# Block 1's VectorE and ScalarE work held in program order, with one weight tile rounded earlier and part of w_in's sums on GpSimd

## The chip, the cores and the metric

The kernel runs on one NeuronCore of a Trainium2 chip. TensorE (PE, with its weight loads as PEld) multiplies, VectorE (DVE), ScalarE (ACT) and GpSimd (POOL) do the rest, and SyncE (SP) issues most DMAs. The metric is device time in microseconds; smaller is better. A difference below 0.3% can't be told from none.

## What is computed

Linear attention without softmax, normalised per row, followed by a two-layer network with a leaky ReLU:

```python
kv = np.einsum('bhsd,bhse->bhde', k, v)        # batch 8, heads 8, seq 576, dim 64
out = np.einsum('bhsd,bhde->bhse', q, kv)
rms = np.sqrt(np.mean(out * out, axis=-1, keepdims=True) + 1e-06)
x = (out / rms * g_norm)                       # then (B,H,S,D) -> (4608, 512)
h = x @ w_in                                   # 512 x 2048, float64 in memory
g = np.maximum(0.01 * h, h)
return g @ w_out                               # 2048 x 512, float64 in memory
```

q, k, v are float32. The two weight matrices come as float64, and the kernel rounds them to float32 itself.

## The kernel before

**Blocks, chunks and slots.** The 4608 rows are nine blocks of 512. The 2048 hidden columns are four chunks (NC = 4), each of two pairs of 128 columns from the lower and the upper half. Block 0 goes first, while weights arrive: `first_block` multiplies chunks 0 to 2 directly, in 12 steps n; step n makes one product with w_in (`h_ps`), applies the leaky ReLU on ScalarE (L1140), and multiplies the result of step n-1 with w_out into four accumulators. Between these, `between(n, 0)` and `between(n, 1)` run what the table `plan` lists for (n, 0) and (n, 1): a number is a weight tile to round, `f` finishes the roundings begun, `t` is a step of the attention of block 0's last rows, `a` a step of block 1's attention, `x` makes block 1's four x sums.

Then comes block 1 with all four chunks, then block 0's chunk 3, then blocks 2 to 8. From here each chunk's two layers are products by Strassen's scheme (seven products instead of eight of half size). Block 1 and block 0's chunk 3 are five units `now` = 0 to 4, each of seven slots, `at` = 7*now + t, 0 to 34. In a slot TensorE makes one first-layer product (8 matmuls of 128x256) and, from slot 9 on, one second-layer product of an earlier unit. First-layer products come in the order 1, 2, 6, 5, 7, 3, 4 and alternate between two banks (h_a and h_c in even units, h_b and h_d in odd ones). A product that accumulates on a bank, or starts it anew, must wait until the last result there has been copied (ScalarE) or added (VectorE): `done` in `product_h`. The seven sides of each product are sums that GpSimd makes: `sides_w1` of w_in, `sides_w2` of w_out, `sums_of` of the activations (tiles gs). Product 6 of the second layer needs the second gs sum.

For blocks 2 to 8 the scheme is applied twice to the first layer, and the weights for that, 49 pieces a chunk, are made once in slots of block 1 and written to DRAM: `combine(c, part)`. Parts 0 and 1 take the sums that `sides_w1` made, parts 2 and 3 w_in's own quarters. The sums of parts 0 and 1 run on GpSimd, those of 2 and 3 on VectorE. `put_off` delays a write by some slots, and `READS` says when the first five pieces are read back into w_in's place (a ring).

**Rounding.** Each of 32 weight tiles (128x512) is loaded raw (512 KB) into one of a few raw homes and rounded in three ScalarE and three VectorE steps that alternate: two reads (L263, L261), a clip (VectorE, L265), ScalarE L270, VectorE L280 and L283. Tiles 24 to 31 are chunk 3's; their homes are the two halves of `early` and the first part of `stage`, in turn. Tiles up to 26 are rounded in `first_block`, the others in slots 0 to 14, one in three slots.

**What sets the order.** The program is traced in one order, and a planner then orders each engine's instructions by its own model of time. An instruction that is pinned stays behind the one traced just before it on its engine. Matmuls, DMAs and roundings are pinned everywhere; in `first_block` attention's work is too, from block 2 on everything; in block 1 (`in_block_1`, set once and never cleared) only GpSimd's sums and the few adds that say so. Block 1's copies, ReLUs and attention steps are the planner's to place. The x sums of block 1 are made in `first_block` and aren't pinned. GpSimd's first instruction after it (L1194) reads the last x sum, so that its sums don't start earlier.

Of the kernel before, what the change touches and what calls it, by code (L numbers as in the profile page):

```python
# [24 lines left out]
def kernel(  # L25
# [70 lines left out]
    def in_turn(ins):  # L96

        if steady or in_line or in_first:
            pin(ins)

    def first_turn(ins):

        if in_first:
            pin(ins)
# [113 lines left out]
    def spare(n, name, dtype=F32):  # L218
# [7 lines left out]
        itertools.cycle([early[:, :NW], early[:, NW:], raws[0]]))  # L226
# [196 lines left out]
    def divide(lo, hi, sums):  # L423
# [3 lines left out]
        for l in range(2):  # L427
# [4 lines left out]
            if l:  # L432
                if in_first:
                    yield
                act = nc.scalar.activation(rms, rms, func=AF.Sqrt, scale=1.0 / D, bias=eps_sb)
                if first_done or in_first:
                    pin(act)
# [58 lines left out]
    def attention(b, apart=True, fine=False):  # L496
# [39 lines left out]
        if KV_BESIDE <= b < B - 1:  # L536
            kv = [(None, None), (0, 1)] if b > KV_BESIDE else [(None, 0), (None, 1)]
        tails = [tail_of(b, max(i * NT, b * S), min((i + 1) * NT, (b + 1) * S),
                         fine or i == b == 1, kv[i - b]) for i in (b, b + 1)]
# [156 lines left out]
    def add(eng, out_, a, b_, minus=False, pinned=False):  # L696
        ins = eng.tensor_tensor(out_, a, b_, op=ALU.subtract if minus else ALU.add)  # L697
        if pinned or steady or (in_block_1 and eng is nc.gpsimd):
            pin(ins)
# [27 lines left out]
    def put_off(to, t):  # L727
        later.append([2 if first_done and in_loop else 1, to, t])
# [8 lines left out]
    def sides_w2(n):  # L737
# [7 lines left out]
        def sums(i):  # L745
# [15 lines left out]
            else:  # L761
# [15 lines left out]
    stage_homes = iter([view(w1_all, (6 + i) * NW, NW) for i in (0, 1)]  # L777
                       + [view(stage, i * NW, NW) for i in (1, 2, 1, 2, 0, 1, 2, 0, 1, 2, 0, 1, 2, 0)])

    def combine(c, part):  # L780
# [5 lines left out]
            [((1, 2), direct)], [((4,), last)]  # L786

        eng = nc.vector if part > 1 else nc.gpsimd
        for js, y in parts[part]:
# [4 lines left out]
            add(eng, s1, y21, y22, pinned=part > 1)  # L794
            add(eng, s2, s1, y11, True, pinned=part > 1)
            add(eng, s3, y11, y21, True, pinned=part > 1)
            add(eng, s4, y12, s2, True, pinned=part > 1)
            to = w1_dram[c][:, :, AT[js[0]]:AT[js[0]] + len(js), :]
            if js[0] == 1:
                for r in range(2):  # L800
                    put_off(to[:, r, :, :], y[:, 0, r, :, :])
            else:
                put_off(to[:, :2, :, :], y[:, 0, :, :, :])
            put_off(to[:, 2, :, :], y22)
            put_off(to[:, 3:, :, :], t)
# [103 lines left out]
    def relu(t, src=None):  # L909
        nc.scalar.activation(t, t if src is None else src, func=AF.Prelu, alpha=SLOPE)  # L910
# [17 lines left out]
    def product_h(n, w_sides, x_sides, to):  # L928
# [3 lines left out]
        def done(i, bank):  # L932

            if i == 1:
                nc.scalar.copy(g11, bank)
            elif i == 5:
                nc.scalar.copy(g22, bank)
# [3 lines left out]
            elif i == 6:  # L941
                nc.scalar.copy(g21, bank)
# [108 lines left out]
    def product_o(n, g_sides, os, finish, second):  # L1051
# [15 lines left out]
        def done(i, bank):  # L1067
# [11 lines left out]
            if c == 0 and fresh:  # L1079
                nc.scalar.copy(to, bank)  # L1080
# [41 lines left out]
    def first_block(between):  # L1122
# [27 lines left out]
        for t in range(4):  # L1150
            o = opool.tile([P, DM], F32, tag="o", name="o", bufs=6)
            if t % 2:
                nc.scalar.copy(o, accs[t])
            else:
                nc.vector.tensor_copy(o, accs[t])
# [8 lines left out]
            (7, 0): (a, a, 17, f), (7, 1): (a, 18, f), (8, 0): (a, 19, f), (8, 1): (a, 20, f),  # L1164
            (9, 0): (a, a, 21, f), (9, 1): (22, a, f), (10, 0): (a, 23, a, f), (10, 1): (a, x),
            (11, 0): (24, f), (11, 1): (25, f), (12, 1): (26, f)}
    loaded, x_sides = 12, None

    def between(n, half):
        nonlocal loaded, x_sides  # L1170
        for what in plan.get((n, half), ()):
# [7 lines left out]
            else:  # L1179
                round_w(what)  # L1180
                to = what + 7 if what < 17 else max(24, what + 3)
# [14 lines left out]
    more()  # L1196
    for part in range(2):
        combine(0, part)
    for part in range(2):
        sides_w2(0)[1](part)  # L1200
    in_loop = True

    LATE_ONE = {17: 2, 19: 1}
    A_SLOTS = {18: 1, 19: 1, 20: 1, 23: 1, 24: 1, 25: 1, 26: 1, 27: 1, 28: 1, 29: 1, 34: 2}
    DIRECT = {15: 0, 16: 1, 20: 2, 21: 3, 22: 4, 23: 5, 26: 6, 27: 7}
    READS = {20: 2, 24: 4, 28: RING}
# [27 lines left out]
    for i, chunks in rounds:  # L1234
        one = i < 2
# [6 lines left out]
        for c in chunks:  # L1242
# [5 lines left out]
            for t in range(7):  # L1248
# [46 lines left out]
                if one:  # L1295
                    if at in DIRECT:
                        combine(DIRECT[at] // 2, 2 + DIRECT[at] % 2)
# [12 lines left out]
                    if loaded < min(rounded + 3, len(w_jobs)):  # L1310
# [6 lines left out]
                    load_some()  # L1317
                    if at == 7 * NC - 4:
                        x_sides, _, sums, _ = sides_x(0)
                    elif at == 7 * N1 - 4:  # L1320
                        x_sides, new_quarters, sums, inner = sides_x(2)
                    if at in (7 * NC - 4, 7 * NC - 3, 7 * N1 - 4, 7 * N1 - 3):
                        go(sums, 2)
                    if at == 7 * N1 - 3:
                        inner(0)
                    elif at == 7 * N1 - 2:
# [45 lines left out]
```

## Time and profile before

| what | us |
|---|---|
| median of 3 runs (lowest, highest) | 930.14 (929.48, 931.88) |
| the profiled execution's own time | 931.65 |
| its span, first to last instruction | 929.9 |
| mean granted TensorE clock | 0.993 of full |

The span is what the profile covers; the execution around it adds 1.75 us. The page lists busy time per engine, then the span in 40 slices. Some landmarks of its timeline: block 0's dense products begin at 23 us, block 1's first product at 111.1 us, block 0's chunk 3 at 216.1 us, block 2 at 242.2 us. One Strassen product, 8 matmuls of 128x256, takes 1.725 us from start to start; a step of `first_block`, 8 matmuls of 128x512, 3.43 us.

### The profile page before, as it was taken

To read this page: it belongs to the slowest core of one execution; us is meant where nothing else is said; L and a number is where in the kernel's file an instruction comes from. 1 tells how busy PE (TensorE), PEld (TensorE's weight loads), DVE (VectorE), ACT (ScalarE), POOL (GpSimd) and SP (SyncE) were. 2 spreads that over 40 slices of the span, in tenths; PEclk is the share of its full clock that TensorE was granted. 3 is DMA by queue.
4 is the path that set the end of the run, shared out by engine and by line. 5 is a ranking of instruction groups with operands and counts; after the bars stand their busy time and mean duration, and the time that the engine had idled before them with its cause. 6 is when DMAs were issued, how large, how long until landed. Compare 5 with 4: busy or idle time off the path is not lost.

```text
span 929.9 us, 18153 instructions
## 1 busy us (share of the span) xinstructions
PE 911.9 (98%) x7024; PEld 788.7 (85%) x7024; DVE 632.4 (68%) x1151; ACT 347.7 (37%) x679; POOL 375.8 (40%) x443
## 2 busy tenths in 40 slices
PE   8999979989999999999999999999999999999998
PEld 5544467878898999999999999999999999999997
DVE  5765855959575877577856786688658755765565
ACT  5756444213234422433333324333343333223330
POOL 2000299844622275226422632255225622552322
PEclk9999989999999999999999999999999999999999
DMA  8997283997689678867886779757765676667632
GB/s 256 249 246 194 68 277 119 278 310 226 207 263 333 203 231 249 256 226 227 250 260 227 219 218 256 243 174 217 242 184 173 188 226 198 185 187 220 199 118 91
DMA packets 92405, 202.16 MB, mean 217 GB/s; under 512 B 10016, under 2 KB 44448, under 8 KB 92320
## 3 DMA queue, kind: packets, MB, share of 16 engines
q1 hardware_dynamic: 81344, 189.14, 68.4%
q10 hardware_dynamic: 10528, 10.69, 3.4%
q8 instruction: 56, 0.92, 0.4%
q0 software_dynamic: 448, 1.18, 0.3%
q14 instruction: 29, 0.24, 0.1%
HBM read 173.44 MB, written 27.53 MB: 216 GB/s over the span
## 4 chain that ended last, share of the span: by engine, by line
PE 85%; DMA 8%; DVE 4%; ACT 2%; issue 1%; POOL 0%; SPq 0%; ACTq 0%; DVEq 0%; POOLq 0%
PE o_c L126 19%; PE o_a L126 18%; PE h_ha L126 11%; PE h_hb L126 10%; PE h_hc L126 8%; PE h_hd L126 8%; PE o_ps L126 3%; PE h_a L126 2%; PE h_c L126 2%; DMA stage<-in_moe_w_out_dram 2%; DMA pairs<-in_moe_w_in_dram 1%; PE h_d L126 1%; PE h_b L126 1%; DMA pairs<-in_v_dram 1%; DMA pairs<-in_moe_w_out_dram 1%
## 5 line engine op out<-in xcount | busy, mean ns | idle before, releaser
L697 POOL TENSOR_TENSOR gs<-g 128x512 f32<-128x512 f32 x66 | 85.2, 1291 | 254.9 <-ACT g L910 254.9
L910 ACT ACTIVATE g<-g 128x512 f32<-128x512 f32 x127 | 80.1, 631 | 143.1 <-DVE g L697 143.1
L1029 ACT COPY w_all<-h_ha 128x512 f32<-128x512 f32 x84 | 49.0, 583 | 169.8 <-PE h_ha L126 164.1
L126 PE MATMUL o_c<-pairs,gs 128*128 128x256 f32 x392 | 93.2, 381 | 0.0
L126 PE MATMUL o_a<-pairs,gs 128*128 128x256 f32 x392 | 93.0, 380 | 0.0
L697 DVE TENSOR_TENSOR o<-h_hb,o 128x128 f32<-128x128 f32 x104 | 29.8, 287 | 83.6 <-ACT pairs L1029 83.5
L126 PEld LDWEIGHTS o_c<-pairs,gs 128*128 128x128 f32 x392 | 71.3, 190 | 9.4 <-POOL pairs L697 1.2
L126 PEld LDWEIGHTS o_a<-pairs,gs 128*128 128x128 f32 x392 | 71.3, 190 | 8.1
L697 DVE TENSOR_TENSOR o<-o_a,o 128x512 f32<-128x512 f32 (+1 forms) x93 | 62.5, 672 | 21.0 <-PE o_a L126 20.6
L697 DVE TENSOR_TENSOR o<-o_c,o 128x512 f32<-128x512 f32 x80 | 54.7, 683 | 27.5 <-PE o_c L126 26.2
L126 PE MATMUL h_ha<-stage,w_all 128*128 128x128 f32 x448 | 59.6, 276 | 0.0
L126 PEld LDWEIGHTS h_ha<-stage,w_all 128*128 128x128 f32 x448 | 56.6, 192 | 3.0 <-issue 0.7
L697 DVE TENSOR_TENSOR g<-g,pairs 128x512 f32<-128x512 f32 x84 | 55.7, 689 | 1.9
L697 POOL TENSOR_TENSOR pairs<-g 128x128 f32<-128x128 f32 x52 | 23.8, 458 | 75.8 <-PE h_hb L126 47.4
L697 DVE TENSOR_TENSOR w_all<-h_hc,w_all 128x512 f32<-128x512 f32 x56 | 38.3, 685 | 15.9 <-PE h_hc L126 15.8
L697 DVE TENSOR_TENSOR o<-h_hd,o 128x128 f32<-128x128 f32 x78 | 22.1, 283 | 38.1 <-ACT pairs L1029 38.0
L126 PE MATMUL h_hb<-stage,w_all 128*128 128x128 f32 x336 | 46.7, 275 | 0.0
L697 POOL TENSOR_TENSOR gs<-gs,g 128x512 f32<-128x512 f32 x33 | 44.3, 1341 | 2.6
L1029 ACT COPY pairs<-h_hb 128x384 f32<-128x384 f32 x84 | 40.1, 477 | 13.8 <-PE h_hb L126 12.9
L697 POOL TENSOR_TENSOR gs<-g,gs 128x512 f32<-128x512 f32 x33 | 45.2, 1369 | 0.0
L126 PE MATMUL o_acc<-w,g 128*128 128x512 f32 x96 | 43.4, 597 | 0.0
L126 PE MATMUL h_hd<-xT,w_all 128*128 128x128 f32 x224 | 43.3, 275 | 0.0
(242 smaller groups left out, 2249.7 us busy)
## 6 DMA issues: line engine op xcount, KB each, us to landing
w_all<-w SPq DMA_DIRECT2D x196, 448.0 KB, 4.2
pairs<-w SPq DMA_DIRECT2D x56, 512.0 KB, 4.3
out_dram<-o ACTq DMA_DIRECT2D x35, 256.0 KB, 4.4
v_in<-in_v_dram SPq DMA_DIRECT2D x27, 288.0 KB, 4.8
k_in<-in_k_dram SPq DMA_DIRECT2D x26, 288.0 KB, 4.4
q_in<-in_q_dram SPq DMA_DIRECT2D x52, 144.0 KB, 5.5
q_in<-in_q_dram SPq DMA_DIRECT2D x52, 140.0 KB, 5.5
w<-stage SPq DMA_DIRECT2D x10, 512.0 KB, 4.1
```

Of the source, the lines that this page charges most:

```text
L126: pin(nc.tensor.matmul(*args, **kw))
L697: ins = eng.tensor_tensor(out_, a, b_, op=ALU.subtract if minus else ALU.add)
L910: nc.scalar.activation(t, t if src is None else src, func=AF.Prelu, alpha=SLOPE)
L1029: nc.scalar.copy(q[:, at], bank)
```

## The change

In block 1 and block 0's chunk 3 (`in_block_1` is now true for these rounds alone, and cleared after them) everything on VectorE and ScalarE is pinned: copies, ReLUs, adds and attention's steps. Tile 24 is rounded in (8, 0) beside tile 19, tile 25 in (10, 1) after the x sums, tile 26 in (11, 0); block 1's attention steps 12 to 14 come one place earlier, and loads are asked for at other steps. Tiles 27 to 31 use the halves of `early` alone, so that all three parts of `stage` hold `combine`'s sums, which before used the place of chunk 3's w_in first. Parts 2 and 3 of `combine` become one, which runs on GpSimd in slots 23, 25, 27 and 29 (before, on VectorE in slots 15 to 27), and its writes are put off by one slot less. w_out's first sums come ahead of `combine` for chunk 0. Attention's steps are spread over other slots, two of its stretches in finer steps; the ring's first reads go from slots 20, 24, 28 to 28, 30, 32, and block 2's x sums one slot later.

```diff
     def in_turn(ins):
-        if steady or in_line or in_first:
+        if steady or in_line or in_first or in_block_1:
             pin(ins)
     def first_turn(ins):
-        if in_first:
+        if in_first or in_block_1:
             pin(ins)
...
         itertools.islice(itertools.cycle(raws), 4 * K * U),
-        itertools.cycle([early[:, :NW], early[:, NW:], raws[0]]))
+        [early[:, :NW], early[:, NW:], raws[0]],
+        itertools.cycle([early[:, :NW], early[:, NW:]]))
...
-                         fine or i == b == 1, kv[i - b]) for i in (b, b + 1)]
+                         fine or i + b in (2, 3) or i == b == 2, kv[i - b]) for i in (b, b + 1)]
...
-        if pinned or steady or (in_block_1 and eng is nc.gpsimd):
+        if pinned or steady or in_block_1:
             pin(ins)
...
-    stage_homes = iter([view(w1_all, (6 + i) * NW, NW) for i in (0, 1)]
-                       + [view(stage, i * NW, NW) for i in (1, 2, 1, 2, 0, 1, 2, 0, 1, 2, 0, 1, 2, 0)])
+    stage_homes = itertools.cycle([view(stage, i * NW, NW) for i in (1, 2, 0)])
...
-            [((1, 2), direct)], [((4,), last)]
-        eng = nc.vector if part > 1 else nc.gpsimd
+            [((1, 2), direct), ((4,), last)]
...
-            add(eng, s1, y21, y22, pinned=part > 1)
-            add(eng, s2, s1, y11, True, pinned=part > 1)
-            add(eng, s3, y11, y21, True, pinned=part > 1)
-            add(eng, s4, y12, s2, True, pinned=part > 1)
+            add(nc.gpsimd, s1, y21, y22)
+            add(nc.gpsimd, s2, s1, y11, True)
+            add(nc.gpsimd, s3, y11, y21, True)
+            add(nc.gpsimd, s4, y12, s2, True)
...
-            put_off(to[:, 3:, :, :], t)
+            put_off(to[:, 3:, :, :], t, 2 - part // 2)
...
-        nc.scalar.activation(t, t if src is None else src, func=AF.Prelu, alpha=SLOPE)
+        first_turn(nc.scalar.activation(t, t if src is None else src, func=AF.Prelu, alpha=SLOPE))
...
-                nc.scalar.copy(g11, bank)
+                first_turn(nc.scalar.copy(g11, bank))
...
-            (7, 0): (a, a, 17, f), (7, 1): (a, 18, f), (8, 0): (a, 19, f), (8, 1): (a, 20, f),
-            (9, 0): (a, a, 21, f), (9, 1): (22, a, f), (10, 0): (a, 23, a, f), (10, 1): (a, x),
-            (11, 0): (24, f), (11, 1): (25, f), (12, 1): (26, f)}
+            (7, 0): (a, a, 17, f), (7, 1): (a, 18, f), (8, 0): (a, 19, 24, f), (8, 1): (a, 20, f),
+            (9, 0): (a, a, 21, f), (9, 1): (22, a, f, a), (10, 0): (a, 23, f, a), (10, 1): (x, 25, f),
+            (11, 0): (26, f)}
...
-                to = what + 7 if what < 17 else max(24, what + 3)
+                to = what + 7 if what < 17 else {23: 26, 25: 28, 26: 28}.get(what, 25)
...
+    sides_w2(0)[1](0)
     for part in range(2):
         combine(0, part)
-    for part in range(2):
-        sides_w2(0)[1](part)
+    sides_w2(0)[1](1)
...
-    LATE_ONE = {17: 2, 19: 1}
-    A_SLOTS = {18: 1, 19: 1, 20: 1, 23: 1, 24: 1, 25: 1, 26: 1, 27: 1, 28: 1, 29: 1, 34: 2}
-    DIRECT = {15: 0, 16: 1, 20: 2, 21: 3, 22: 4, 23: 5, 26: 6, 27: 7}
-    READS = {20: 2, 24: 4, 28: RING}
+    LATE_ONE = {15: 2, 16: 2, 17: 1, 18: 1, 19: 2}
+    A_SLOTS = {18: 1, 19: 2, 22: 1, 23: 1, 24: 1, 25: 1, 26: 1, 27: 1, 28: 2, 29: 1, 30: 1, 31: 2,
+               34: 2}
+    DIRECT = {23: 0, 25: 1, 27: 2, 29: 3}
+    READS = {28: 2, 30: 4, 32: RING}
...
-        one = i < 2
+        one = in_block_1 = i < 2
...
-                    if loaded < min(rounded + 3, len(w_jobs)):
+                    if loaded < min(rounded + 2, len(w_jobs)):
...
-                    load_some()
+                    load_some(2 if at in (19, 20) else 1)
```

Left out are the same edit on the other copies, and the shift of block 2's x sums.

## The prediction

> **What bounds the kernel now.** I read the page first, for where TensorE is not working, then the windows from 110 us on, then the order of instructions around each hole.
>
> ```profile
> span 929.9 us, 18153 instructions
> PE 911.9 (98%) x7024; PEld 788.7 (85%) x7024; DVE 632.4 (68%) x1151; ACT 347.7 (37%) x679; POOL 375.8 (40%) x443
> PEclk9999989999999999999999999999999999999999
> 114.00:117.00 3.00, 0.69 (x4) 0.26 (x2) 2.90 (x4) 1.36 (x3) 3.00 (x3) 1.00 0.48 129
> ...
> 120.00:123.00 3.00, 0.00 (x0) 0.00 (x0) 3.00 (x3) 1.50 (x3) 2.92 (x4) 0.98 0.60 171
> 123.00:126.00 3.00, 2.23 (x5) 1.85 (x6) 2.41 (x4) 0.75 (x2) 3.00 (x3) 0.50 1.03 343
> ...
> 110.40:178.40 68.00, 58.73 (x275) 49.21 (x275) 46.59 (x55) 28.79 (x53) 65.79 (x59) 0.92 0.64 202
> 196.80:211.90 15.10, 13.49 (x121) 11.55 (x122) 10.01 (x24) 1.84 (x3) 0.00 (x0) 0.89 0.74 248
> ```
>
> In a window the columns are length, then busy time (count) of PE, PEld, DVE, ACT, POOL, then granted clock, DMA share, GB/s. TensorE is busy for 98% of the span: it is the bound, and only its holes can be won. From 23 us to 111 us and from 201 us on it runs without a gap but at the very end. Between lie four holes, each ended by a late VectorE or ScalarE instruction, three of them followed by half clock. And GpSimd is busy for 65.8 of 68 us up to 178 us, then idle for 15 us: near a limit in the first half of the stage, free in the second.
>
> ```profile
> 104.41 0.60 ACT L1140 ACTIVATE g<-h_ps 128x512 f32<-128x512 f32 x1 [0.66 <-PE h_ps L126]
> 109.49 0.68 DVE L697 TENSOR_TENSOR xt<-xT,xt 128x512 f32<-128x512 f32 x1
> 110.40 0.18 POOL L1194 COPY pairs<-xt 1x1 f32<-1x1 f32 x1 [104.00 <-PE o_acc L126]
> 117.29 0.57 ACT L935 COPY g<-h_a 128x512 f32<-128x512 f32 x1
> 123.03 0.68 DVE L697 TENSOR_TENSOR g<-h_c,g 128x512 f32<-128x512 f32 x1
> 144.67 1.27 POOL L697 TENSOR_TENSOR gs<-gs,g 128x512 f32<-128x512 f32 x1
> 197.58 0.68 DVE L697 TENSOR_TENSOR g<-h_d,g 128x512 f32<-128x512 f32 x1
> 198.41 3.43 PE L126 MATMUL h_d<-xt,pairs 128*128 128x256 f32 x8 [2.99 <-DVE g L697]
> ```
>
> The timeline shows why. Product 1 (h_a) ends at 112.8 us, but its copy starts at 117.29, behind rounding; TensorE, which accumulates on the same bank, stands from 114.69 to 117.95 (3.26). Product 2 (h_c) ends at 114.69, its add runs at 123.03: TensorE stands from 119.92 to 123.77 (3.85). The same happens in chunk 1 (140.76 to 142.92, 2.16) and in chunk 3 (195.42 to 198.41, 2.99; the add of 197.58 had its product at 190). Idle: 12.26 us. After these holes 16 matmuls (normal 3.45 us) took 6.47, then 5.24, then 8 (normal 1.73) took 3.27: half clock cost 3.0 + 1.8 + 1.5 = 6.3 us. All there is to win is 18.6 us.
>
> **What the Trainium skill says.** "TensorE: Matmul & The Clock Gate", What's actually happening: the array falls to half rate after an idle window of about 3.4 us. The clock here agrees: 0.50 in stretches of 6.8, 3.4 and 3.4 us, the second after a hole of only 2.16 us. The same page, Architectural detail, calls ScalarE's and VectorE's queues strict FIFO; the trace agrees, since the add at 123.03 was ready for 5 us behind others' work. "SBUF — State Buffer", Who interferes with whom: a VectorE tensor_tensor with both inputs in SBUF contends with GpSimd's reads. Agreed: a sum for w_in 128x256 took 0.42 us on VectorE with GpSimd idle (209 us), 1.49 beside it (167 us); GpSimd's 128x512 took 1.28 to 1.72.
>
> **The change, part by part.**
>
> *Tile 24 beside 19, 25 and 26 a stage earlier.* In slot (8, 0) ScalarE reads tile 24's raw data, which landed at 86.28; ScalarE got there at 85.6. I walk both queues, each instruction when its engine and input are free, with before's durations and start-to-start spacings (ScalarE 0.55, VectorE 0.60 us). Tile 24's two reads end at 87.6, the conversions of 19 and 24 at 88.7; the squares of attention's second half start at 88.6 (before 87.11); VectorE's sums 90.8 (88.19), transposes 94.4 (92.74), reciprocal 101.65 (100.06). The next step is taken one place earlier, so the first inv is at 102.6 (103.0); after tile 23 the second is at 107.25 (106.48) and the last of the four x sums ends at 110.9 (110.17). Block 0's activation of product 10 stands behind that spread: 103.6 at the end, needed at 104.21; covered by 0.6 us.
>
> Product 11's is not. Tile 25 is now rounded in (10, 1), ahead of it on ScalarE, and its VectorE step stands behind the x sums: 110.9 + 0.41 (clip) + 0.63 (ScalarE) + 0.58 (activation) = 112.4. TensorE wants that activation at 107.64; before, it ended at 105.0. So a new wait of 4.8 us, with half clock after it: 1.4 to 3.1 us from the two sizes of gated stretch, I take 2.1. Block 0 ends at 112.4 + 3.45 + 2.1 = 118.0 instead of 111.1.
>
> *What hides it.* GpSimd starts when the x sums end, not when block 0 does: 110.9 instead of 110.2. From there to the second gs sum, which product 6 of the first second-layer product needs, it has the same 30 sums in another order: 110.40 to 145.94, nearly gapless. Unstretched they would take 14 x 1.28 + 16 x 0.73 = 29.6 us; the 5.9 us more lie beside 17 VectorE operations, 0.35 each. Three of those are gone (two of tile 24, one of 25), so 1.0 comes back of the 0.7 lost: 145.7 to 146.7. TensorE's work from slot 0 to that product is 14 groups of 1.725 = 24.15 us; from 118.0 that is 142.1, plus waits.
>
> *Held order in slots 0 to 11.* The copy of product 1 now stands behind tile 26 and two copies of the accumulators, not behind 27: 119.8, right at its product's end. The add of product 2 stands behind tile 27's clip: 123.3, with TensorE there at 123.2. Each tile's chain (0.56 + 0.68 ScalarE, 1.0 to 1.5 clip, 0.65, 1.0 to 1.3, 1.1 to 1.6 VectorE, about 5.5 us) fits three slots of 1.725 just about, so slot 9 begins at about 135.3 and TensorE reaches the gs-bound product at 143.9: GpSimd sets it, at 146.4, against 149.89 before. Gain 3.5; for a wait of 2.5 us that may cost half clock once (before, 2.16 us cost 1.8) I take off 0.5: 3.0.
>
> *Held order later.* In slot 22 the add of product 2 now comes first; the hole at 195.42 and its half clock go: 2.99 + 1.54 = 4.5 us. What is late next there? The second-layer adds have two slots (6.9 us) of slack, transposes wait for q tiles that land at some 185 and 189 (loads moved into slots 19 and 20, two at a time), used near 188 and 191.
>
> *Last sums on GpSimd.* Per chunk 4 x 0.73 + 4 x 0.46 (128x256 and 128x128 rows) = 4.8 us, four times 19.2 us, to 27 if contended by 1.4. Queued behind them are the gs sums of chunk 3 and the inner x sums of block 2. From 196.8: two combines, w2 sums (2.6), a third combine, two gs sums: 216.5 to 222, wanted near 222 to 224. Inner sums end at 237.5 to 240.5, wanted at 241. GpSimd's idle time (15.2 and 13.3 us in the trace) hides it; without that cover, up to 3 us. VectorE loses 32 sums, off the path, worth nothing more.
>
> *One stage home instead of w_in's last places, one load ahead less, reads of ring at 28, 30, 32.* The next raw tile now queues on SP behind writes that wait for GpSimd until 131, lands by 138, wanted at 139; the one after by 142, wanted at 149. Ring reads land some 20 us before block 2. Finer attention steps move the same work: zero. If the raw tile is late, ScalarE stands and chunk 1 with it: up to 3 us, in the range.
>
> Sum: -3.0 - 4.5 = -7.5 us. The span becomes 922.4, the profiled execution 924.2 from 931.65; the runs shown have median 930.14, 1.5 below it, so 922.6.
>
> **Rivals.**
> - *Neither GpSimd nor half clock holds TensorE.* It arrives at 143.9 and goes on: -6.0 - 4.5 = -10.5, 919.6. For it: GpSimd's stretching is a matter of luck. Against: it needs half of the 5.9 us of stretching to vanish (unstretched, the sum would be there at 140.7).
> - *GpSimd late in slots 23 to 34, or one gain lost.* Only one of the two gains stays, or 3 us are given back at block 2: -3 to -4.5, 926. Against: its idle 28 us.
> - *Slower: block 0's end is pure cost.* The wait of the activation behind tile 25 is 4.8 us plus half clock for two stretches, 3.4: 8.2 us. If the early waits belong to the rounding's data and not to its order, slots 0 to 11 repeat before's 14.1 us of loss (9.3 idle, 4.8 half clock), and against 8.2 stand only the 4.5 of chunk 3: +3.7, 933.8. It decides when less than 3.7 of those 14 us goes. For it: tile chains of 5.5 us in 5.2 us of slots, VectorE busy 2.9 of 3 us at 114. Against: the add of 123.03 had nothing to wait for.
> - *It about cancels*: both halves of the above, within 0.3%.
>
> **Chances.** Forecast 0.45, own range 920 to 925; more 0.10; less 0.17; no change 0.08; slower 0.20. A difference of 0.3%, 2.8 us, is what a measurement of this kernel tells from none. Faster 0.72, same 0.08, slower 0.20. The range goes to 918 and to 933: it leaves out most of the slower case and the tail of the best.
>
> **What would show it.** Right: block 0's last activation ends near 112.4 with TensorE idle for some 4.8 us before it and clock 0.50 after; GpSimd's copy at 111; the first product that reads gs from GpSimd at 146 to 147, released by GpSimd; no hole in chunk 3; from there the same spacing 7.5 us earlier. Wrong: that product at 150 or later, a hole before a product whose add or copy waits behind rounding, GpSimd's gs sums late near 222, or no wait at 107.6.

## The result, and the profile after

The changed kernel takes 930.01 us (median of 12 executions, 926.63 to 933.39) beside 931.95 for the kernel before on the same chip: ratio 0.9982, 95% interval 0.9965 to 1.0. That is less than can be told from no change: 1.9 us, where the forecast was 7.5 less (922.6). The two profiled executions took 930.66 and 931.65 us.

From the page of the changed kernel:

```profile
span 929.0 us, 18151 instructions
...
PE 910.7 (98%) x7024; PEld 785.7 (85%) x7024; DVE 610.2 (66%) x1119; ACT 347.5 (37%) x679; POOL 390.6 (42%) x475
```

TensorE is as busy as before. The 32 sums have moved: VectorE lost 22.2 us, GpSimd gained 14.8. So what was won in one place must have been lost in another, and the windows of the changed kernel say where (length, busy time and count of PE, PEld, DVE, ACT, POOL, then granted clock, DMA share, GB/s):

```profile
109.00:114.40 5.40, 0.01 (x1) 0.00 (x0) 4.63 (x8) 1.14 (x3) 1.16 (x2) 0.93 0.34 97
114.40:120.90 6.50, 6.47 (x8) 2.71 (x9) 5.73 (x5) 2.21 (x4) 6.42 (x5) 0.54 0.00 0
147.20:149.85 2.65, 0.08 (x2) 0.01 (x1) 1.29 (x2) 0.63 (x1) 2.57 (x3) 1.00 0.63 218
149.85:156.80 6.95, 6.95 (x24) 5.84 (x25) 0.69 (x1) 1.22 (x2) 6.71 (x7) 0.75 0.16 53
...
196.80:211.90 15.10, 15.10 (x148) 12.35 (x147) 8.49 (x13) 3.80 (x8) 13.68 (x19) 1.00 0.94 275
```

TensorE stands at the end of block 0 (109.0 to 114.4) and then runs at about half clock; it stands again before 149.85, with a clock of 0.75 after; chunk 3 (196.8 to 211.9) now has no hole and full clock, where before TensorE was busy for 13.49 of 15.10 us at 0.89; and in block 2 there is a hole at 246.4 (the last line of the timeline below) that the kernel before didn't have. The timeline of the changed kernel names what ended each wait (start, length, engine, line, operation; in brackets the idle time before it and its releaser; SPq is SP's issuing of DMAs):

```profile
88.06 0.67 ACT L264 ACTIVATE add<-early 128x512 uint32<-128x512 uint32 x1 [2.09 <-DMA early<-in_moe_w_out_dram]
...
113.12 0.18 POOL L1193 COPY pairs<-xt 1x1 f32<-1x1 f32 x1 [106.72 <-DVE xt L698]
...
113.80 0.58 ACT L1139 ACTIVATE g<-h_ps 128x512 f32<-128x512 f32 x1
...
114.43 1.22 PE L126 MATMUL o_acc<-w,g 128*128 128x512 f32 x1 [5.42 <-ACT g L1139]
...
122.92 0.58 ACT L934 COPY g<-h_a 128x512 f32<-128x512 f32 x1 [1.20 <-PE h_a L126]
...
123.98 0.68 ACT L262 ACTIVATE cut<-early 128x512 f32<-128x512 f32 x1
124.68 2.17 SPq L237 DMA_DIRECT2D early<-in_moe_w_in_dram  x4
...
128.88 2.90 SPq L735 DMA_DIRECT2D w<-pairs  x3
...
134.21 1.28 POOL L698 TENSOR_TENSOR pairs<-w_all 128x512 f32<-128x512 f32 x1 [2.06 <-DMA w<-pairs]
...
149.85 0.70 PE L126 MATMUL o_a<-pairs,gs 128*128 128x256 f32 x2 [2.57 <-POOL gs L698]
...
240.62 0.73 POOL L698 TENSOR_TENSOR stage<-xT 128x256 f32<-128x256 f32 x1 [11.25 <-DMA w<-stage]
...
248.04 0.94 PE L126 MATMUL h_ha<-stage,w_all 128*128 128x128 f32 x6 [1.67 <-POOL stage L698]
```

Read from the top: ScalarE stood 2.09 us on tile 24's landing; GpSimd started at 113.12; block 0's last activation ended at 114.4, and TensorE had waited 5.42 us for it. The first product of the second layer that reads a gs sum of GpSimd (product 6; `o_a<-pairs,gs`) began at 149.85, against 149.89 before: nothing won there, and it was GpSimd that released it. In its row of sums GpSimd had stood 2.06 us on a DRAM write of `pairs`, which SP issued only after a load that waited for ScalarE's last reading of tile 27 (123.98). In block 2 it was GpSimd's inner x sums that came late, behind writes of `stage`.

What SP's queue itself waited for, from the waits of the changed kernel (first for 112 to 126 us, then for 225 to 250; total, times, longest):

```profile
SPq L237 <- ACT cut L262: 13.8, 1, 13.8
...
SPq L735 <- DMA out_dram<-o: 15.3, 2, 10.9
```

SP stood for 13.8 us at the head of block 1 on that reading, and for 15.3 us in block 2 on stores of block 1's outputs, issued on ScalarE's queue.

The accounts of the two profiled executions, by marks that both have:

| stretch | before | after | difference | forecast |
|---|---|---|---|---|
| start to product 6 of the second layer | 149.89 | 149.85 | -0.04 | -3.5 |
| from there to slot 13 (half clock) | 5.18 | 6.97 | +1.79 | +0.5 |
| slot 13 to slot 34 (chunk 3) | 82.82 | 78.13 | -4.69 | -4.5 |
| slot 34 to the second-layer product of slot 37, in block 2 | 13.91 | 15.89 | +1.98 | 0 |
| the rest of the execution | 679.85 | 679.82 | -0.03 | 0 |
| sum | 931.65 | 930.66 | -0.99 | -7.5 |

### The profile page after: what moved, and what is told of

It is laid out like the page before. It is cut to its first block, busy times and chain, and to the rows that moved or that the text cites. A ratio compares the mean times of both kernels' runs of the same rounds, so it can differ in the third digit from the quotient of the medians.

```text
span 929.0 us, 18151 instructions
## 1 busy us (share of the span) xinstructions
PE 910.7 (98%) x7024; PEld 785.7 (85%) x7024; DVE 610.2 (66%) x1119; ACT 347.5 (37%) x679; POOL 390.6 (42%) x475
## 4 chain that ended last, share of the span: by engine, by line
PE 82%; DMA 9%; POOL 3%; DVE 3%; issue 1%; ACT 1%; SPq 0%; POOLq 0%; ACTq 0%; DVEq 0%
PE o_c L126 19%; PE o_a L126 18%; PE h_ha L126 11%; PE h_hb L126 10%; PE h_hc L126 8%; PE h_hd L126 8%; DMA pairs<-in_moe_w_in_dram 3%; PE o_ps L126 3%; DMA stage<-in_moe_w_in_dram 2%; POOL stage L698 2%; PE h_a L126 2%; POOL pairs L698 1%; PE h_c L126 1%; DMA pairs<-in_v_dram 1%; PE h_b L126 1%
## 5 line engine op out<-in xcount | busy, mean ns | idle before, releaser
L126 PE MATMUL o_acc<-w,g 128*128 128x512 f32 x96 | 46.7, 632 | 6.0 <-ACT g L1139 6.0
L698 DVE TENSOR_TENSOR o<-h_hd,o 128x128 f32<-128x128 f32 x78 | 22.2, 284 | 38.1 <-ACT pairs L1028 38.0
L1193 POOL COPY pairs<-xt 1x1 f32<-1x1 f32 x1 | 0.2, 177 | 106.7 <-DVE xt L698 106.7
```

What stands on the lines that cost most here:

```text
L126: pin(nc.tensor.matmul(*args, **kw))
L1193: pin(nc.gpsimd.tensor_copy(pair(0, NW)[:1, :1], x_sides[4][:1, 0, :1]))
```

## The experiments

Theory G: GpSimd's row of 30 sums, from the end of block 1's x sums (the copy at L1193) to the second gs sum, sets product 6; whatever TensorE waits for before that is covered. Its rivals: TensorE's own waits set it (theory A), or the held order wasn't what made or ended the waits (theory R). Theory Q concerns block 2, theories S and L what delays the row. All kernels compute the whole result. The kernel before, timed beside each of them, had medians between 931.95 and 932.38 us.

"Start" is GpSimd's copy that opens the row, "row" the time from there to the end of the second gs sum, "rest" the profiled execution's time less the start of product 6. The six columns on the right are of one profiled execution each.

| kernel | median us (executions) | ratio to before, 95% interval | tile 24 landed | ScalarE's wait for it | start | row | product 6 | rest |
|---|---|---|---|---|---|---|---|---|
| before | | | 86.28 | | 110.40 | 35.54 | 149.89 | 781.76 |
| the change | 930.01 (12) | 0.9982 [0.9965, 1.0] | 87.97 | 2.09 | 113.12 | 36.67 | 149.85 | 780.81 |
| 1 tile 25 behind the activation | 927.64 (17) | 0.9962 [0.9949, 0.9975] | 90.29 | 4.00 | 115.46 | 34.91 | 150.43 | 779.12 |
| 2 tiles 24 to 26 back | 929.53 (22) | 0.9985 [0.9975, 0.9995] | 88.03 | none | 110.68 | 39.32 | 150.05 | 779.02 |
| 3 held order alone | 935.15 (9) | 1.0039 [1.0025, 1.0052] | 86.93 | none | 110.42 | 36.20 | 146.68 | 787.86 |
| 4 without held order | 934.93 (22) | 1.0025 [1.001, 1.0039] | 90.20 | 3.63 | 115.35 | 36.12 | 151.53 | 784.14 |
| 5 w_out's sums back | 929.58 (9) | 0.9977 [0.996, 0.9995] | 85.22 | none | 110.83 | 36.46 | 147.34 | 779.06 |
| 6 last sums a slot earlier | 929.47 (22) | 0.9971 [0.9959, 0.9984] | 87.35 | 1.72 | 112.50 | 37.00 | 149.56 | 778.92 |
| 7 = 1 + 5 + 6 | 926.80 (22) | 0.9954 [0.994, 0.9968] | 89.22 | 2.90 | 114.37 | 35.01 | 149.43 | 780.23 |
| 8 = 2 + 5 + 6 | 924.84 (6) | 0.9928 [0.9909, 0.9946] | 87.89 | none | 110.83 | 36.38 | 147.26 | 777.22 |
| 9 writes of pair(0) first | 929.07 (22) | 0.9969 [0.9955, 0.9984] | 93.48 | 3.74 | 118.65 | 35.49 | 154.20 | 780.75 |
| 10 = 8 + 9 | 923.88 (5) | 0.9907 [0.9888, 0.9926] | 86.09 | none | 110.56 | 35.91 | 146.53 | 777.18 |
| 11 = 6 + 9 | 926.07 (7) | 0.994 [0.9918, 0.9963] | 90.87 | 4.12 | 116.03 | 35.48 | 151.56 | 778.93 |
| 12 = 10, outputs free | 924.16 (6) | 0.9925 [0.9897, 0.9953] | 87.75 | none | 110.29 | 36.11 | 146.45 | 777.15 |
| 13 tile 24 one step later | 928.76 (5) | 0.996 [0.9946, 0.9974] | 87.78 | none | 112.52 | 37.01 | 149.58 | 780.64 |
| 14 = 13 + 6 + 9 | 924.84 (5) | 0.9914 [0.99, 0.9928] | 85.66 | none | 111.63 | 34.70 | 146.39 | 778.45 |

In all of them but the kernel before, product 6 begins 0.05 or 0.06 us after the second gs sum: there the releaser is always GpSimd. And in all 16 profiles GpSimd goes through its row of 30 sums without standing for longer than 0.15 us, but for one wait on a DMA write of `pairs` in seven of them. So none of TensorE's waits stands inside the row.

### The early rounding and the held order

**1. Tile 25 behind block 0's last activation**, to take away its wait of 5.4 us:

```diff
-            ... (10, 1): (x, 25, f),
-            (11, 0): (26, f)}
+            ... (10, 1): (x,),
+            (11, 0): (25, f), (11, 1): (26, f)}
```

> Changed kernel, but tile 25 is rounded in (11, 0), behind the last block-0 activation, and tile 26 in (11, 1). Theory G (GpSimd's chain of sums, which starts when the x sums end, sets the second-layer product 6, and TensorE's wait at block 0's end lies in its shadow): the 5.4 us wait before the last o_acc goes, block 1 begins near 111.5 instead of 120.9, but product 6 of the second layer still starts near 149.5 to 150; the time stays within 1.5 us of the changed kernel's 930.0. Theory A (that wait and its half clock are a pure loss): product 6 comes 5 to 9 us earlier, time 921 to 925.

The wait before block 0's last product is gone (0.42 us in its place at 111), and product 6 came at 150.43. From this kernel's timeline:

```profile
122.87 0.45 PE L126 MATMUL h_a<-xt,pairs 128*128 128x256 f32 x1 [3.98 <-issue]
...
150.43 0.91 PE L126 MATMUL o_a<-pairs,gs 128*128 128x256 f32 x3 [1.35 <-POOL gs L698]
```

But this doesn't show what 5 us of TensorE's waiting are worth, because they came back: TensorE now stands 3.98 us at 118.89, since slot 0's copy on ScalarE (122.18) stands behind the roundings, and it runs at half clock after that. It reaches product 6 at 149.08, later than in the change (147.27), and even so stands 1.35 us for GpSimd. Nor is the unmoved time of product 6 a constant: the row started 2.3 us later than in the change, since tile 24 landed later, and was 1.8 us shorter, without a write wait. The median is still 2.4 us lower than the change's; in the profile the difference lies behind product 6 (rest 779.1 in place of 780.8), where after this shorter hole no half clock follows. Theory G had allowed a change of 1.5 us.

**2. Tiles 24 to 26 and attention's steps in the places of before**:

```diff
-            ... (8, 0): (a, 19, 24, f), (8, 1): (a, 20, f),
-            (9, 0): (a, a, 21, f), (9, 1): (22, a, f, a), (10, 0): (a, 23, f, a), (10, 1): (x, 25, f),
-            (11, 0): (26, f)}
+            ... (8, 0): (a, 19, f), (8, 1): (a, 20, f),
+            (9, 0): (a, a, 21, f), (9, 1): (22, a, f), (10, 0): (a, 23, a, f), (10, 1): (a, x),
+            (11, 0): (24, f), (11, 1): (25, f), (12, 1): (26, f)}
```

> Changed kernel, but tiles 24 to 26 and block 1's last attention steps have their places of before. Theory G: the x sums end near 110.3 instead of 112.9, GpSimd starts 2.7 us earlier, product 6 near 147; time 2 to 4 us below the changed kernel: 926 to 928. Theory A: the wait of 5.4 us goes as well, 921 to 925. If the rounding of 24 to 26 beside block 1's first products is what stalled them (theory R): the copies and adds of slots 0 to 3 are late again by 3 us each, product 6 stays near 150, 930 or more.

GpSimd started at 110.68, 2.4 us before the change, and gave it all back, most of it at one place. GpSimd in this kernel's timeline:

```profile
134.43 1.27 POOL L698 TENSOR_TENSOR pairs<-w_all 128x512 f32<-128x512 f32 x1 [3.85 <-DMA w<-pairs]
```

This sum, the 17th of the 30 (the expectation of experiment 9 calls it the 19th), overwrites pair(0), and may not until the writes that read it have landed: it stands 1.8 us longer than in the change. The numbers are those of theory R, with a hole of 7.88 us at 115 behind a late copy and product 6 near 150. That the hole isn't the cause can be seen from GpSimd, for which TensorE still stands 2.57 us at product 6, and from experiment 8, where a hole of 6.8 us stays and product 6 moves.

**3. The kernel before with the held order alone** (`in_block_1` as in the change, all else as before; block 0's output copies stay free):

```diff
-        if steady or in_line or in_first:
+        if steady or in_line or in_first or in_block_1:
...
-        one = i < 2
+        one = in_block_1 = i < 2
```

> Kernel before, with only the held order of VectorE and ScalarE in block 1; last sums on VectorE, tiles and slots as before. Theory G: product 6 waits for GpSimd, near 146 to 147 (149.9 before), so 3 us gained there; the hole of chunk 3 (195.4) goes, 4.5 us, unless the last sums on VectorE now stand in the way; 923 to 927. Theory R (the order was not what made the waits): within 2 us of before, 930 to 932.

The first half holds: product 6 at 146.68, 3.2 us before its time in the kernel before. The second doesn't. With VectorE's 32 last sums in held order, block 0's chunk 3 gets a hole of its own, from the timeline:

```profile
210.72 0.41 DVE L697 TENSOR_TENSOR stage<-w_all 128x256 f32<-128x256 f32 x1
211.16 1.37 DVE L697 TENSOR_TENSOR stage<-stage,w_all 128x256 f32<-128x256 f32 x1
212.45 1.48 DVE L697 TENSOR_TENSOR stage<-w_all 128x256 f32<-128x256 f32 x1
213.85 1.48 DVE L697 TENSOR_TENSOR stage<-w_all,stage 128x256 f32<-128x256 f32 x1
...
215.68 1.09 PE L126 MATMUL o_ps<-qT,kv 64*32 64x384 f32 x8 [5.53 <-DVE kv L370]
```

Attention's copy of kv stands behind four sums, three of them stretched from 0.41 to some 1.4 us beside GpSimd's gs sums. The rest is 6.1 us longer than before, and the kernel is slower by 0.39%. So the order alone, with the last sums left on VectorE, gives back more than it brings.

**4. The change without the held order in block 1** (the lines of experiment 3 taken back, and `add`'s too):

> Changed kernel without the held order in block 1 (the planner's order again, everything else as changed). Theory G: the start of GpSimd's chain stays at 113, holes of 2 to 4 us with half clock come back in chunks 0, 1 and 3: 934 to 940. Theory R: within 2 us of the changed kernel.

4.9 us slower than the change. An add waits behind rounding, TensorE stands 2.40 us for it from 156.98 to 159.38 and loses clock after. That is the one hole of the expected kind, in chunk 1: chunk 0 has none over 0.5 us, and chunk 3 none at all. From this kernel's timeline:

```profile
196.45 0.69 DVE L698 TENSOR_TENSOR g<-h_d,g 128x512 f32<-128x512 f32 x1 [1.10 <-PE h_d L126]
```

This is chunk 3's add that was late in the kernel before (197.58 there); here VectorE waits for TensorE's product and not the other way round, without the held order. The order is worth keeping for chunk 1; the gain in chunk 3 doesn't need it.

### The waits on writes

**5. w_out's first sums back behind combine**:

```diff
-    sides_w2(0)[1](0)
     for part in range(2):
         combine(0, part)
-    sides_w2(0)[1](1)
+    for part in range(2):
+        sides_w2(0)[1](part)
```

> The changed kernel with both parts of w_out's sums for chunk 0 put back behind combine's sums on GpSimd, as before; nothing else. Theory G (GpSimd's row of 30 sums, which starts when the inner x sums end, sets the second gs sum and with it product 6 of block 1's second layer): the 2.06 us that GpSimd waited at 134.21 for the DRAM write of pairs is gone, the row takes 34.6 to 36.2 us from its start, so with the start at 112.9 to 115.4 the second gs sum ends at 147.5 to 149.5 if tile 24 lands as early as in the changed kernel (149.79 there), the hole ahead of product 6 falls from 2.57 us to under 1 and no half clock follows it: 1.5 to 3 us less, 927.0 to 928.5 us. Rival (TensorE's own late start at 120.94 sets it, the GpSimd wait was beside it): product 6 stays within 0.5 us of 149.85 and the time at 930.

A miss: the order of the sums wasn't what made the write late. GpSimd in the timeline:

```profile
131.71 1.28 POOL L698 TENSOR_TENSOR pairs<-w_all 128x512 f32<-128x512 f32 x1 [1.85 <-DMA w<-pairs]
```

The row is as long as in the change (36.46). Product 6 came earlier in this profile because the row started earlier: tile 24 had landed at 85.22, before ScalarE came to it at 85.67. The median stayed where it was.

**6. The last part of combine one slot earlier**, so that its writes stand ahead of block 1's output stores:

```diff
-    DIRECT = {23: 0, 25: 1, 27: 2, 29: 3}
+    DIRECT = {22: 0, 24: 1, 26: 2, 28: 3}
```

> The changed kernel with combine's last part issued one slot earlier each (slots 22, 24, 26, 28 in place of 23, 25, 27, 29), so that the DRAM writes of chunk 3's stage sums stand in SP's queue ahead of the writes of block 1's outputs. Theory Q (the inner x sums wait for those stage writes, which wait in SP's queue behind the output stores): the hole of 1.67 us at 246.4 goes or falls under 0.5 us, GpSimd no longer stands 11 us at 240.6 behind a DMA of stage, and product 1 of block 2's second layer that waits for it comes 1.7 to 2.2 us earlier; 927.8 to 928.4 us. Rival (the x sums are late for GpSimd's own work or the reads of the next weights): the hole stays within 0.4 us of 1.67 and the time at 930.

The hole at slot 37 is gone, and the stretch behind product 6 shrank from 780.81 to 778.92 us: theory Q, 1.9 us. In one point it was wrong: GpSimd still stands there on a DMA, but once and for less long, and SP's wait for the output stores is still there, now ahead of reads for block 2. GpSimd in the timeline:

```profile
238.56 0.73 POOL L698 TENSOR_TENSOR stage<-xT 128x256 f32<-128x256 f32 x1 [9.77 <-DMA w<-stage]
```

The median fell by only 0.5, within the uncertainty of two such medians: the spread of the executions (925.19 to 933.07) hid it, and what made that spread was still open.

**7 and 8. Combinations**: 7 is 1 + 5 + 6, 8 is 2 + 5 + 6.

> Both edits together, and tile 25 rounded behind block 0's last activation, 26 one step later. By theories G and Q: from the 927.6 us that late rounding of tile 25 alone gave, no write wait is left on GpSimd to take away (its row of sums there started at 115.46 and took 34.9 us), so only the 2.0 us of the hole at slot 37 go: 925.3 to 926.2 us, product 6 at 150 to 150.5 as there. Rival (the waits only move): 927.6 us or more.

> Both edits together, with tiles 24 to 26 and the attention steps in the places of before. By theory G GpSimd starts at 110.2 to 110.7 and, with no wait for the write of pairs (3.85 us at 134.43 when tile 24 was put back alone), ends the second gs sum at 145.5 to 147.0 in place of 150.0; with the hole at slot 37 gone as well that is 5 us less than the 929.5 us of tile 24 put back alone: 924.0 to 925.5 us. Rival (TensorE's start behind the long hole at 115 to 123 sets product 6, or the waits only move): product 6 at 148.5 or later, 927 us or more.

8 came as theory G had it: start 110.83, product 6 at 147.26, 924.84 us, although TensorE stands for 6.8 us at 115 and runs at half clock for 5.8 us after. 7 came 0.6 us above its range: its row started 3.5 us later than that of 8.

The plainest support for theory G is 8 beside 5. Both rows start at 110.83; they end at 147.29 in 5 and 147.21 in 8. TensorE gets to product 6 at 144.77 in 5 and at 146.49 in 8, 1.7 us apart, and product 6 begins at the same time but for 0.08 us. From the timelines of 5 and of 8:

```profile
147.34 0.48 PE L126 MATMUL o_a<-pairs,gs 128*128 128x256 f32 x1 [2.57 <-POOL gs L698]
...
147.26 0.48 PE L126 MATMUL o_a<-pairs,gs 128*128 128x256 f32 x1 [0.78 <-POOL gs L698]
```

**9. Only the two writes of pair(0) one slot earlier**, ahead of the load of tile 29 in SP's queue:

```diff
-    def put_off(to, t, slots=2):
-        later.append([slots if first_done and in_loop else 1, to, t])
+    def put_off(to, t, slots=2, first=1):
+        later.append([slots if first_done and in_loop else first, to, t])
...
-                put_off(to[:, :2, :, :], y[:, 0, :, :, :], 2 - part // 2)
-            put_off(to[:, 2, :, :], y22, 2 - part // 2)
+                put_off(to[:, :2, :, :], y[:, 0, :, :, :], 2 - part // 2, min(part, 1))
+            put_off(to[:, 2, :, :], y22, 2 - part // 2, min(part, 1))
```

> The changed kernel, and only the two DRAM writes of pair(0) (chunk 0's products 5 and 6) are issued one slot earlier, at slot 0, ahead of the load of raw tile 29 in SP's queue. Theory S: with the order held, ScalarE's last reading of tile 27 stands behind block 0's output copies and slot 0's copy (123.98 us in the changed kernel), the load of tile 29 waits for it at the head of SP's queue to 124.68, the writes of pair(0) behind it are issued at 129.66 and 130.52 and land at 134.05, and GpSimd's 19th sum waits for them from 132.15. With the writes issued by 123 they land before 128, the wait is gone, the second gs sum ends 34.5 to 35.5 us after GpSimd's start (36.7 in the changed kernel), product 6 comes 1.2 to 2.1 us earlier at the same start, its hole falls from 2.57 us to about 1 and the half clock behind it may go: 926.5 to 928.5 us. Rival (GpSimd's row is set by its own sums and VectorE's claim on the memory, the write wait was beside them): the row stays at 36.2 us or more, 929.5 to 930.5 us.

From the timeline:

```profile
118.65 0.18 POOL L1193 COPY pairs<-xt 1x1 f32<-1x1 f32 x1 [112.23 <-DVE xt L698]
...
121.92 0.91 SPq L735 DMA_DIRECT2D w<-pairs  x2
129.51 1.75 SPq L237 DMA_DIRECT2D early<-in_moe_w_in_dram  x4
```

The writes are now issued 7.6 us ahead of the load, and the write wait is gone: the row takes 35.49 us in place of 36.67. That is what theory S named, 1.2 us. But the time missed its range (929.07). The profiled execution shows what can stand against the gain: tile 24 landed at 93.48, the row began at 118.65, product 6 at 154.20, and it took 934.95 us. Behind product 6 it agrees with the change to 0.06 us; what was gained in the row was lost in the start of it. It is one of the two slowest of 22, so it doesn't explain the median.

**10 to 12.** 10 is 8 + 9; 11 is 6 + 9, the change with SP's order mended twice and its roundings left in place; 12 is 10 with block 0's output copies free again ("the second kernel" in its expectation is 10):

```diff
-                first_turn(nc.scalar.copy(o, accs[t]))
+                nc.scalar.copy(o, accs[t])
             else:
-                in_turn(nc.vector.tensor_copy(o, accs[t]))
+                nc.vector.tensor_copy(o, accs[t])
```

> The version with tiles 24 to 26 in before's places, w_out's sums behind combine and combine's last part a slot earlier (924.84 us), with the writes of pair(0) one slot earlier as well. Theory S: only 0.54 us of write wait were left there, so product 6 moves from 147.26 to 146.5 to 147.0 and the time to 924.2 to 924.9 us. Rival (the earlier writes hold up SP's loads): a new wait in slots 4 to 9 and 925.5 us or more.

> The changed kernel with the two edits of SP's order and nothing else: writes of pair(0) at slot 0, combine's last part at slots 22 to 28. Theories S and Q add up: 1.2 to 2.1 us at product 6, up to 1.75 of half clock behind it where that goes, and 1.7 to 2.2 at slot 37 (929.47 us was measured with the last alone): 925.5 to 927.8 us. Rival (the gains hide each other or move): 929 us or more.

> As the second of these four, with block 0's output copies free as before, not held in program order. They ran at 112 us where they were free and at 120.3 behind two roundings where they were held, and slot 0's copy, for which TensorE waits 6.8 us from 115.1, stands behind them. Theory G (GpSimd's row sets product 6): the hole at 115 shrinks by 1 to 4 us, the hole ahead of product 6 grows by as much, and the time stays within 0.7 us of the second kernel's. Rival (TensorE's start sets it): 2 to 3 us less.

10 has the lowest median, 0.9907 of before (0.9888 to 0.9926), an interval clear of the change's own; from those of 8, 12 and 14 it can't be told. 11 shows that the two mends of SP's order bring 930.01 down to 926.07 us with nothing else touched. That is more than the two gave apart (0.5 and 0.9 us); no run shows why. 12 doesn't tell the theories apart: freeing the copies turned the hole of 6.83 us at 115 into two of 3.27 and 3.84 us, and TensorE got to product 6 at the same time (145.11 beside 145.17). Product 6 stayed (146.45 beside 146.53), as did the median.

### The start of the row

By then the table showed it: where tile 24 is rounded beside 19 and ScalarE waits for it, GpSimd starts 25.15 to 25.17 us after tile 24's landing, in seven profiles of seven; in the six with tile 24 behind the x sums it starts between 110.29 and 110.83, wherever between 86.1 and 88.0 the tile landed. Whether the wait for the landing or tile 24's own work does it, one profile tells, that of experiment 5, where tile 24 is beside 19 and had landed before ScalarE came:

```profile
85.67 0.73 ACT L264 ACTIVATE add<-early 128x512 uint32<-128x512 uint32 x1
...
110.83 0.18 POOL L1193 COPY pairs<-xt 1x1 f32<-1x1 f32 x1 [104.41 <-DVE xt L698]
```

The row starts within 0.6 us of the six: in that place the work itself costs next to nothing, and the landing nearly all. Two more kernels were made for the question.

**13. Tile 24 one step later, beside tile 20**, and **14, the same with 6 and 9**:

```diff
-            ... (8, 0): (a, 19, 24, f), (8, 1): (a, 20, f),
+            ... (8, 0): (a, 19, f), (8, 1): (a, 20, 24, f),
```

> The changed kernel with tile 24 rounded beside tile 20 in (8, 1), one step later than beside 19; nothing else. Theory L (ScalarE, first in first out, stands on tile 24's landing at 88 to 93, and all of block 1's attention and the x sums behind it): one step is 3.5 us, tile 24 has mostly landed when ScalarE gets to it, ScalarE's wait there falls from 2.1 to 4.1 us to under 1, and GpSimd starts at 110.5 to 112 in place of 112.5 to 118.7, for most landings up to 91. The median falls by 2 to 3 us to 927 to 928, and the spread of the executions (6.8 us in the changed kernel) falls too. Rival (tile 24's own work ahead of the x sums delays them, about 2.5 us of ScalarE and VectorE): GpSimd starts at 112.5 or later though ScalarE doesn't wait for the landing, and the time stays at 929.5 to 930.5.

> The same with the two edits of SP's order (writes of pair(0) at slot 0, combine's last part at slots 22 to 28; 926.07 us with tile 24 beside 19). Theory L: 2 to 3 us less than that, 923.3 to 924.5 us, which would be the forecast's own size reached with block 0's 5.4 us of wait still there. Rival (tile 24's work, not its landing): 925.7 to 926.5 us.

ScalarE in the timeline of 13 reads tile 24 without a wait, 3.2 us after its landing:

```profile
90.95 0.69 ACT L264 ACTIVATE add<-early 128x512 uint32<-128x512 uint32 x1
```

Both theories are half right. The row starts at 112.52 and 111.63, not at 110.3 to 110.8: in this place tile 24's work ahead of the x sums costs 0.8 to 2.2 us, which the rival says; beside 19 it did not (experiment 5). But ScalarE doesn't wait for the landing in either profile, and the executions spread less: five of 14 lie within 1.5 us (923.72 to 925.22), while seven of 11 spread over 6.4. These are few executions, and experiment 12, with tile 24 behind the x sums, also had one of six at 930.72. The medians fell by some 1.2 us, from the change to 13 (928.76) and from 11 to 14, where theory L had 2 to 3; both lie above its ranges. In 14's profile product 6 hardly waits: its weights stood 0.53 us on GpSimd, its matmuls on nothing:

```profile
146.38 0.73 PEld L126 LDWEIGHTS o_a<-pairs,gs 128*128 128x128 f32 x4 [0.53 <-POOL gs L698]
146.39 0.92 PE L126 MATMUL o_a<-pairs,gs 128*128 128x256 f32 x3
```

This is the forecast's own picture: product 6 at 146.4, TensorE and GpSimd arriving together, chunk 3 without a hole, 924.84 us beside the 924.2 forecast for the profiled execution, and block 0's wait of 5.2 us still there. It took three edits the change doesn't have. One thing is outside the picture: behind product 6 this execution took 1.3 us longer than those of 8, 10 and 12, with a hole of 1.17 us at 271.5, where TensorE waited for a DMA into `pairs`; no other profile has it. And kernels 8, 10 and 12, with tiles 24 to 26 where they were before, are as fast: the early rounding itself buys nothing that shows here.

## Why the prediction was wrong

*The new wait at block 0's end* was forecast as 4.8 us and measured as 5.42, with half clock after it (the forecast's sum for the activation, 112.4, should read 112.5). Product 10's activation, "covered by 0.6 us", left TensorE 0.60 us idle at 104.71, and TensorE reached product 6 at 147.27, not 143.9. That all this would be covered was right: TensorE still stood 2.57 us there for GpSimd.

*GpSimd's row sets product 6*: right as a mechanism, wrong in both terms, 3.46 us in all.
- The start, forecast at 111 (110.9 in the sum): 113.12. The step that failed is "tile 24's raw data, which landed at 86.28; ScalarE got there at 85.6". I took one execution's landing for a constant and counted 0.7 us of waiting; it was 2.09 in the profile of the change, 1.7 to 4.1 in six others, and none in experiment 5, where the tile landed at 85.22 and the row started at 110.83, as forecast. Of the 2.2 us in the change 1.7 are the later landing (87.97), the rest the walk behind it. ScalarE's queue is first in first out, as the Trainium skill says ("TensorE: Matmul & The Clock Gate", Architectural detail) and as 88.06 shows, so all of block 1's attention and its x sums wait with it. A load that landed in time in its old place had become a bound in the new one.
- The row, forecast as 35.4 us ("the same 30 sums in another order"): 36.67. The step that failed is the one on stage homes and loads: "the next raw tile now queues on SP behind writes". It is the other way round: the writes queue behind a load that waits for a raw home until ScalarE has read tile 27, and that reading now stands behind slot 0's copy. I had asked whether the tile would be late and not who stands behind it in SP's queue; experiment 9 shows the 1.2 us.

*Half clock after the wait at product 6*: I took off 0.5 us; 1.79 were lost. The hole was 2.57 us, as forecast (2.5), but half clock comes in whole steps of 3.4 us or not at all (last section), here 1.7 us or nothing.

*Chunk 3*: forecast -4.5, measured -4.69. The size was right; the reason, "in slot 22 the add of product 2 now comes first", is one that the gain doesn't need. In the kernel before that add stood behind four of combine's sums on VectorE, here the first and the last of them; the add follows at 197.58:

```profile
196.07 0.87 DVE L697 TENSOR_TENSOR stage<-w_all 128x128 f32<-128x128 f32 x1
...
197.38 0.28 DVE L697 TENSOR_TENSOR stage<-w_all,stage 128x128 f32<-128x128 f32 x1
```

With these sums on GpSimd there is no hole here even without the held order (experiment 4). With the order and the sums on VectorE the hole at this place shrinks to 0.55 us, but the stretch from slot 13 to slot 34 takes 5.9 us longer than before (experiment 3). So the 32 sums, which the forecast called "off the path, worth nothing more", were on it. Two parts of the change act on this hole, and the forecast credited one of them alone; that its size came out is partly luck. Experiment 4 also has the change's other slots for attention, so their share isn't separated.

*Last sums on GpSimd*: taken as hidden, with "up to 3 us" if the cover goes. The sums themselves were in time: the last ended at 229.4. Late were their writes to DRAM, 12 us later, in SP's queue behind block 1's output stores; the inner x sums wait for the same places in `stage`. 1.98 us, of which experiment 6 took back 1.89. I had walked the sums and not the DMAs that they issue.

The rival "only one gain stays" came nearest. Its two halves, "only one of the two gains" and "3 us are given back at block 2", were given as alternatives and happened together. The 0.08 on no change was too little.

Open: why the issue of tile 24's load varies from execution to execution, and why SP waits at those places for stores that another engine's queue carries. No run here was made for either. Nor is it known why tile 24 costs more one step later, beside 20, than beside 19. And its landing came at 85.2 to 93.5 us in the eight profiles with tile 24 beside 19, at 86.1 to 88.0 in the six with it behind the x sums; whether the change itself delays the load or these eight were unlucky is not settled.

## What to carry to other kernels

Before an instruction is moved ahead of others on a first-in-first-out engine, look at when its input lands over several executions, since everything behind it inherits that time. When sums or copies are moved, follow their DMAs through the issuing queue to the next owner of the buffer: a load that waits for a free home holds up every write behind it. A wait in front of a stage costs nothing while another engine's row ends later; and when it is taken away, look whether it comes back at the next product, as it did twice here, before anything is concluded. Find the row that ends last and shorten that.

## What the runs showed of the hardware

- The same hole of 2.57 us before product 6 was followed by 3.4 us of half clock in the change and in experiments 9 and 11, but not in 2 and 5 (from product 6 to slot 13: 6.97 us in the change, 5.29 in 5), nor was one of 2.78 us in 4, nor one of 3.26 us at 114.69 in the kernel before. A hole of 2.00 us in 14 was followed by it too, holes of 1.28 to 1.36 never. The Trainium skill speaks of an idle window of about 3.4 us that runs freely ("TensorE: Matmul & The Clock Gate", What's actually happening); here holes shorter than that were enough, and the same hole could go either way.
- Which way it goes can be worked out from the clock records of the 16 traces, from 24 us on and the programs' ends aside. In each of them half clock begins on a fixed grid with steps of 3.41 us (113.61 and 151.16 us in the change are 11 steps apart) and lasts one, two or three steps. Before each of the 28 times that it set in, TensorE had been idle for at least 2.00 us of the step just ended; in no step at full clock after which it stayed away was TensorE idle for more than 1.93 us. In the change 2.10 us of the hole of 2.57 us lay in one step (from 147.75 to 151.16). In 5 the grid cut the same hole into 0.65 and 1.92 us, and in the kernel before it cut the one of 3.26 us into 1.35 and 1.91. The grid lies elsewhere in each execution, so where a hole falls on it is chance.
- Tile 24's load was issued between 76.5 and 85.4 us and landed 7.2 to 8.7 us later, over the 16 profiles. In the seven where ScalarE waited for it, the start of GpSimd's row followed its landing to 0.02 us.
